# Queries and keys of batches 0 and 1 read in long runs, and the first layer's weights rebuilt two tiles at a time

## The chip, the cores and the metric

One core of one Trainium2 chip runs the whole kernel. The metric is the time of one execution on the device in microseconds. Before the change it was 829.93 us, the median of 3 runs (829.26 to 830.01). The profile comes from one further execution of the same program.

## The reference

Attention over 4 batches, 8 heads, 576 positions and 64 values per head feeds two layers of the same form. The attention adds a coarse part (queries, keys and values averaged by fours, a full softmax over 144 groups, repeated four times) and a local part (each position sees the three before and the three after it).

```python
q_d = q.reshape(B, H, Sd, factor, D).mean(axis=3)        # factor 4; k and v the same
out_up = np.repeat(sm_attn(q_d, k_d, v_d), factor, axis=2)
mask = np.abs(pos[:, None] - pos[None, :]) < factor
scores = np.where(mask, scale * q @ k.T, -1e9)
out = out_up + softmax(scores) @ v                       # float32
x = moe(out)      # h = x @ w_in;  max(0.01 h, h) @ w_out
x = moe2(x)       # h = x @ w_in;  a squared ramp of h;  @ w_out
```

There are 2304 rows; w_in is 512 by 2048 and w_out 2048 by 512, in both layers. q, k and v come as float32, the four weights as float64, of which the kernel reads the two 32-bit words.

## The kernel before

**The two layers.** The rows are cut into four blocks of 512 and one of 256. A weight is held as two float16 tiles (a high part and a remainder), and each product is three float16 products on PE. The first layer runs `g1` (L1939, x by w_in) and `g2` (L2203, by w_out) in steps of 12 products; one step of `g1` takes one of the 16 column tiles of w_in. The second layer (L1969, L2039, L2139) trades products for sums on DVE.

**A weight tile** is rebuilt in `weight` (L632): a DMA brings 64-bit words into a buffer (L667), DVE shifts and joins them in three instructions (L686, L692, L698) into a float32 tile of 512 elements, ACT rounds that to the high part (L723) and DVE takes the remainder (L756). There are 16 such tiles of w_in and 16 of w_out in the first layer. From the third tile of w_in on, one DMA already brings two tiles, but each is rebuilt by itself.

**The attention of batches 0 and 1** (of batch 1 the first 448 positions, for the local part) works on transposed queries and keys. `prep` (L1157) loads, for each batch and each of four pairs of heads, the queries and keys by blocks of 64 positions, with one DMA for each head (L1172): 64 partitions by 9 runs of 64 floats. `tr` (L1203) turns each block, both heads at once, by a transposing product with the identity: 64 partitions by 128 columns, nine of them, five into one bank of PSUM and four into another. `tr_c` (L1221, L1233) copies each bank to SBUF on ACT. The scores (L1512) and the products with the values (L1572) follow; the coarse part sums the transposed queries and keys by fours on DVE (L1310) and has its own scores (L1351), transposes (L1402) and products (L1420). The rest of the attention is done on DVE with rows on partitions (L1707 to L1816).

**The order** of all instructions is worked out while the program is built. Each piece of work is an entry with an engine, a duration, the buffers and banks that it needs and the entries that it waits for; a planner walks through time and gives each engine the ready entry of the lowest key. Engines issue strictly in that order. Where the plan finds nothing ready for PE up to 140 us of its own time, it writes a product of zeros into a spare bank (`fill`, L2548): 128 by 512, whose result is not used. There are 80 of these. The numbers of the plan that the change touches are the largest count of weight loads open at a time (AHEAD), the spacing of the attention's due times (HP_GAP), the priority of the local attention of later blocks (RUSH_P), and the assumed durations of the transposing products and of their copies.

The other way to load queries and keys stands in the program already, behind `b in RUNS`, with `RUNS = ()`, so that no batch uses it:

```python
if b in RUNS:
    nc.sync.dma_start(
        out=st[nm].ap[:QB].rearrange("p (h x) -> p h x", h=2),
        in_=src[b, 2 * hp:2 * hp + 2].rearrange("h (i n) d -> i h (n d)", n=QBB))
```

Of the kernel before, what the change touches and what calls it, by code (L numbers as in the profile page):

```python
# [59 lines left out]
RUSH_P = 8  # L60
# [16 lines left out]
RUNS = ()  # L77
# [23 lines left out]
HP_GAP = 0.8  # L101
# [3 lines left out]
TWO_FROM = {1: 2, 2: 99}  # L105
# [3 lines left out]
AHEAD = 4  # L109
# [300 lines left out]
def kernel(  # L410
# [138 lines left out]

    def per_step(blk):  # L550
        return BLK // tokens(blk)
# [69 lines left out]
    w_in[1] = [w1_rows[:, i].rearrange("p f (c n) -> p f c n", c=KDM) for i in range(2)]  # L621
# [10 lines left out]
    def weight(m, which, f, due):  # L632
        st = {}
        hi, lo = (e[:, f] for e in (w_in, w_out)[which][m])
        if which == 0:
            hi, lo = (e.rearrange("p c n -> p (c n)") for e in (hi, lo))
            src = w_src[m][0].rearrange("(c p) n -> p c n", p=P)[:, :, f * P:(f + 1) * P]
        else:
            src = w_src[m][1][f * P:(f + 1) * P, :]

        two = which == 0 and f >= TWO_FROM[m]
        second = two and (f - TWO_FROM[m]) % 2 == 1
        n_load = 2 if two else 1
        if second:
            st = w_two[m, f - 1]
        if which == 0:
            w_two[m, f] = st

        lead = LEAD_W if m == 2 else (LEAD_W1, LEAD_W1O)[which] + (W1_MORE if f >= W1_FROM else 0)
        ch = Chain(due, lead, 512 + (0 if second else 1024 * n_load), hold=RESERVE_W, early=m == 1)  # L650
        ch.window = WINDOW_W if m == 2 else WINDOW
        if m == 1 and f < W1_RUSH:
            ch.rush = RUSH

        def load():
            w_open[0] += n_load
            w_begun[m] += n_load
            st["s"] = buf(1024 * n_load, m == 1)
            st["users"] = n_load
            t = st["s"].ap.bitcast(I32)  # L660
            if which == 0:
                t = t.rearrange("p (c n) -> p c n", c=KDM)
                s = w_src[m][0].rearrange("(c p) n -> p c n", p=P)
                s = s[:, :, f * P:(f + n_load) * P].bitcast(I32)
            else:
                s = src.bitcast(I32)
            nc.sync.dma_start(out=t, in_=s)  # L667

        def words():
            a = st["s"].ap.bitcast(I32)  # L670
            if which == 0:
                a = a.rearrange("p (c n t) -> p c n t", c=KDM, t=2)
                a = a[:, :, P:] if second else a[:, :, 0:P]
                return a[:, :, :, 0], a[:, :, :, 1]
            a = a.rearrange("p (n t) -> p n t", t=2)
            return a[:, :, 0], a[:, :, 1]

        def f32(i32=False):
            a = st["f", f].ap
            a = a.bitcast(I32) if i32 else a  # L680
            return a.rearrange("p (c n) -> p c n", c=KDM) if i32 and which == 0 else a


        def c1():
            st["f", f] = buf(512, m == 1)
            nc.vector.tensor_scalar(  # L686
                out=f32(True), in0=words()[1], scalar1=3, scalar2=0x3FFFFFF8,
                op0=ALU.logical_shift_left, op1=ALU.bitwise_and,
            )

        def c2():
            nc.vector.scalar_tensor_tensor(  # L692
                out=f32(True), in0=words()[1], scalar=-0x40000000, in1=f32(True),
# [3 lines left out]
        def c3():  # L697
            nc.vector.scalar_tensor_tensor(  # L698
                out=f32(True), in0=words()[0], scalar=29, in1=f32(True),
# [3 lines left out]
        def loaded():  # L703
            st["users"] -= 1
            if not st["users"]:
                st["s"].free()
            w_open[0] -= 1

        late = (m, which) == (2, 1)
        if not second:  # L710
            o = ch.op("SP", DMA, load, [w_last[f - W_EARLY]] if late and f >= W_EARLY else [],
                      need=(1024 * n_load,),
                      lat=LAT_W[which] * n_load)
            o.gate = lambda: w_open[0] < AHEAD and (
                m == 1 or w_begun[1] == 2 * KFF and o.key <= sch.step + WINDOW_W
                and (which == 1 or arena.close_spare())
            )
            st["load"] = o
        old = [w_last[f]] if late else []
        ch.op("DVE", t_dve(512, True), c1, [st["load"]], need=(512,))  # L720
        ch.op("DVE", t_dve(512), c2)
        ch.op("DVE", t_dve(512), c3, after=(loaded,))
        ch.op("ACT", t_act(512), lambda: nc.scalar.activation(  # L723
            out=hi, in_=st["f", f].ap, func=AF.Copy, scale=SW), ch.ops[-1:] + old)
        free = (lambda: st["f", f].free(),)
        if m == 1 and f < LO_PE[which]:

            def low():
                ps = st["ps"] = banks.get()
                nc.tensor.matmul(ps, ident_w, st["f", f].ap, start=True, stop=False)  # L730
                nc.tensor.matmul(ps, ident_n, hi, start=False, stop=True)

            ch.op("PE", dict(dur=5 * t_mm(512), cols=5 * 512), low, banks=1, mlp=True,
                  after=free)
# [1849 lines left out]
```

## Time and profile before

| what | value |
|---|---|
| median of 3 runs | 829.93 us |
| profiled execution, its own time | 827.44 us |
| its span, first to last instruction | 825.7 us |
| PE busy | 815.7 us (99%) |
| DVE busy | 723.9 us (88%) |
| ACT busy | 488.5 us (59%) |
| DMA busy share, 0 to 40 us | 0.93 |
| packets under 512 bytes | 36062 of 74155 |

The busy time of PE counts every product, those of zeros too, and the ends of its products are modelled: a product of 512 columns is shown some 380 ns long, while in a row they start about 216 ns apart. So a share of 99% says that PE's stream has almost no holes, not that all of it is wanted work. What a group of products costs is read from where it starts to where the next group starts.

### The profile page before, as it was taken

What the parts mean: (1) busy time and instruction counts of PE and PEld (TensorE: products, weight loads), DVE (VectorE), ACT (ScalarE), POOL (GpSimd) and SP (SyncE); (2) the same over time, 40 slices, a digit from 0 to 9 for tenths busy, and PEclk for the clock granted to TensorE, in tenths of its full rate; (3) what the DMA queues carried; (4) which work ended last, traced back from release to release, by engine and by line L of the source; (5) the groups of instructions that cost most, each with busy time, mean ns of one, the idle gap of its engine ahead of it and who ended that gap; (6) DMA issues with size and microseconds to landing.
All of it is one profiled execution on the core that took longest, in us unless ns stands there. A gap on an engine that the chain in (4) does not pass through costs nothing. (4 is left out here: it accounts for less than half of the span.)

```text
span 825.7 us, 16297 instructions
## 1 busy us (share of the span) xinstructions
PE 815.7 (99%) x6244; PEld 542.8 (66%) x6244; DVE 723.9 (88%) x1347; ACT 488.5 (59%) x1258; POOL 38.9 (5%) x60
## 2 busy tenths in 40 slices
PE   8999999999999999999999999999999999999998
PEld 5765555444454445444447886766888888889997
DVE  5997999999999999999999999998598598858661
ACT  5977676473633564363545557776677576746640
POOL 2001000051002400000000000000000000000000
PEclk9999999999999999999999999999999999999999
DMA  9988746693226703401512333000100000000001
GB/s 153 181 196 189 221 148 208 169 171 60 58 68 160 118 1 92 126 1 51 154 52 102 103 109 108 40 1 1 52 1 15 23 18 2 14 27 14 2 21 58
DMA packets 74155, 67.88 MB, mean 82 GB/s; under 512 B 36062, under 2 KB 57950, under 8 KB 74078
## 3 DMA queue, kind: packets, MB, share of 16 engines
q1 hardware_dynamic: 62878, 62.69, 27.3%
q0 software_dynamic: 11200, 4.15, 4.4%
q8 instruction: 49, 0.80, 0.4%
q14 instruction: 28, 0.23, 0.1%
HBM read 62.08 MB, written 4.72 MB: 81 GB/s over the span
## 5 line engine op out<-in xcount | busy, mean ns | idle before, releaser
L1939 PE MATMUL bank<-arena,w 128*128 128x512 f16 (+1 forms) x960 | 197.3, 358 | 0.0
L2203 PE MATMUL bank<-arena,w 128*128 128x512 f16 (+1 forms) x912 | 193.1, 362 | 0.0
L1939 PEld LDWEIGHTS <-w 128*128 128x128 f16 x960 | 92.9, 98 | 88.5 <-issue 1.0
L2203 PEld LDWEIGHTS <-w 128*128 128x128 f16 x960 | 92.1, 98 | 87.2 <-issue 2.3
L2139 PEld LDWEIGHTS <-arena 128*128 128x128 f16 x930 | 90.7, 98 | 10.4
L1969 PEld LDWEIGHTS <-w 128*128 128x128 f16 x960 | 86.3, 98 | 14.0 <-issue 2.6
L1969 PE MATMUL bank<-arena,w 128*128 128x256 f16 (+1 forms) x768 | 93.2, 269 | 1.1 <-DVE bank L2019 0.6
L2139 PE MATMUL bank<-w,arena 128*128 128x256 f16 x600 | 75.3, 273 | 0.0
L2052 ACT ACTIVATE arena<-bank 128x512 f32<-128x512 f32 x67 | 39.7, 592 | 55.6 <-PE bank L1939 52.5
L1969 PEld LDWEIGHTS <-arena 128*128 128x128 f16 x720 | 64.8, 98 | 9.9 <-issue 0.4
L1969 PE MATMUL bank<-arena 128*128 128x256 f16 (+1 forms) x576 | 66.9, 264 | 0.2 <-DVE w L2064 0.2
L2182 DVE SCALAR_TENSOR_TENSOR arena<-arena 128x512 f16<-128x512 f32 x69 | 47.0, 684 | 2.6 <-ACT arena L2178 2.6
L2064 DVE SCALAR_TENSOR_TENSOR w<-w,bank 128x512 f32<-128x512 f32 x50 | 33.8, 681 | 17.6 <-ACT w L2060 17.2
L2056 ACT ACTIVATE w<-bank,half 128x512 f32<-128x512 f32 x50 | 34.2, 684 | 22.6 <-DVE bank L2019 19.3
L2178 ACT ACTIVATE arena<-arena 128x512 f16<-128x512 f32 x69 | 43.4, 629 | 1.2 <-DVE arena L1816 0.3
L2001 ACT COPY w<-bank 128x256 f32<-128x256 f32 x100 | 34.2, 366 | 15.5 <-PE bank L1969 14.7
L1782 DVE TENSOR_TENSOR arena<-arena 128x768 f32<-128x768 f32 (+2 forms) x60 | 41.1, 688 | 1.4
L2105 ACT ACTIVATE arena<-arena 128x256 f16<-128x256 f32 (+1 forms) x62 | 33.1, 556 | 13.2 <-DVE arena L2064 5.6
L1707 DVE TENSOR_TENSOR arena<-arena 128x1792 f32<-128x1792 f32 x20 | 40.2, 2016 | 0.6 <-issue 0.3
L2139 PE MATMUL bank<-arena 128*128 128x256 f16 x330 | 40.4, 273 | 0.0
L1715 DVE TENSOR_REDUCE arena<-arena 128x28 f32<-128x1792 f32 x20 | 40.1, 2009 | 0.0
L1763 ACT ACTIVATE arena<-arena 128x64 f32<-128x64 f32 x140 | 35.5, 338 | 7.6 <-DVE arena L1746 7.6
(251 smaller groups left out, 1335.3 us busy)
## 6 DMA issues: line engine op xcount, KB each, us to landing
arena<-in_moe_w_in_dram SPq DMA_DIRECT2D x15, 1024.0 KB
arena<-in_moe_w_out_dram SPq DMA_DIRECT2D x8, 1024.0 KB
arena<-in_moe_w_out_dram SPq DMA_DIRECT2D x10, 512.0 KB
w<-in_moe_w_out_dram SPq DMA_DIRECT2D x6, 512.0 KB
arena<-in_k_dram SPq DMA_DIRECT2D x23, 112.0 KB
arena<-in_v_dram SPq DMA_DIRECT2D x23, 112.0 KB
arena<-in_k_dram SPq DMA_DIRECT2D x16, 144.0 KB
out_dram<-w SPq DMA_DIRECT2D x9, 256.0 KB
```

The source lines that it names most:

```text
L1707: nc.vector.tensor_tensor(pv(par, j0), st["q", par].ap.rearrange("p (j d) -> p j d", d=D)[:, j0:j0 + JC, :] .unsqueeze(2).to_broadcast([P, ...
L1715: nc.vector.reduce_sum(sv(par)[:, j0:j0 + JC, :], pv(par, j0), axis=AX)
L1763: nc.scalar.activation(out=pr[:, j, w, :], in_=va[:, j0 + j + w, :], func=AF.Copy, scale=sv(par)[:, j0 + j, w:w + 1],)
L1782: nc.vector.tensor_tensor(out, x, y, op=ALU.add)
L1939: nc.tensor.matmul(h[:, e], a[:, f, c, :] if m == 1 else a[:, f // FP, c, f % FP], y[:, :, c, :], start=(n == 0), stop=(n == 3 * KDM - 1),)
L1969: nc.tensor.matmul(o[:, e], a[:, i, c], y[:, k, c, :], start=first and e == 0 and n == 0, stop=n == 5, skip_group_check=True,)
L2001: nc.scalar.copy(side(p, nm), part(p, t, j))
L2052: nc.scalar.activation(out=t, in_=st["h", p], func=AF.Prelu, scale=s_in * sg, alpha=0.01)
L2139: nc.tensor.matmul(o[:, k], a[:, i, at:at + P], y[:, j], start=opens and p == e == k == n == 0, stop=p == PH - 1 and e == E - 1 and n == 2 ...
L2178: nc.scalar.activation(out=gv(p)[0], in_=st["t", p].ap, func=AF.Copy, scale=so)
L2182: nc.vector.scalar_tensor_tensor(out=lo, in0=st["t", p].ap, scalar=so, in1=hi, op0=ALU.mult, op1=ALU.subtract)
L2203: nc.tensor.matmul(o, a, y[:, e, :], start=(first and n == 0 and c % E == 0), stop=(last and n == 2), skip_group_check=True,)
```

## The change

It does three things in the program, and gives the planner other numbers. First, `RUNS = (0, 1)`: for batches 0 and 1 partition i receives positions 9i to 9i+8 of both heads, in runs of 2304 bytes, by one DMA instead of two. The block that `tr` turns then holds every ninth position, and one head of it is turned by one ordinary product with the identity into its half of the bank's partitions, so that there are two products where one transposing product was. The copy on ACT writes the positions back in order (steps of nine). Second, tiles 2 to 15 of w_in of the first layer are rebuilt two at a time, by instructions of 1024 elements; w_in lies in another order in SBUF for that. Third, the lines that add 1e-9 and take the reciprocal become one helper, with the same instructions.

```diff
-RUSH_P = 8
+RUSH_P = 20
-RUNS = ()
+RUNS = (0,1)
+RUN_PE = 0.045
+RUN_ACT = 1.5
-HP_GAP = 0.8
+HP_GAP = 1.0
-TWO_FROM = {1: 2, 2: 99}
+TWO_FROM = (2, 98)
-AHEAD = 4
+AHEAD = 6
...
-    def weight(m, which, f, due):
+    def weight(which, f, n, due):
...
+        size = 512 * n
...
         def c1():
-            st["f", f] = buf(512, m == 1)
+            st["f"] = buf(size, True)
             nc.vector.tensor_scalar(
-                out=f32(True), in0=words()[1], scalar1=3, scalar2=0x3FFFFFF8,
+                out=f32(), in0=words()[1], scalar1=3, scalar2=0x3FFFFFF8,
...
-                        nc.tensor.transpose(
+                        nc.tensor.matmul(
                             ps[par * D:(par + 1) * D, (n - n0) * QB:(n - n0 + 1) * QB],
-                            a[:, par, n, :], ident[:QB, :QB]
+                            a[:, par, n, :], ident[:QB, :QB], start=True, stop=True,
                         )
...
-                t = ch.op("PE", pe_tr(QB, n * (2 if b in RUNS else 1), QB), ...
+                t = ch.op("PE", pe_mm(RUN_PE * 2 * n, QB, 2 * n, P) if b in RUNS else pe_tr(QB, n, QB), ...
-                c = ch.op("ACT", t_act(n * QB, True), ...
+                c = ch.op("ACT", t_act(n * QB, True) * (RUN_ACT if b in RUNS else 1), ...
...
+    for which, late in ((0, 0.0), (1, 1.5)):
+        f = 0
+        while f < KFF:
+            n = 2 if f >= TWO_FROM[which] else 1
+            weight(which, f, n, step_of[1, b0, f // per_step(b0)] + late)
+            f += n
```

PE's first rows after its opening products of zeros (nine before the change, seven after), first of the kernel before; L1216 is the transposing product, L2548 the zeros.

```order
L1216 MATMUL bank_64<-ident,w_61 128x64 x5
L2548 LDWEIGHTS zeros
L2548 MATMUL bank_63<-zeros 128x512
L2548 LDWEIGHTS zeros
L2548 MATMUL bank_63<-zeros 128x512
L2548 LDWEIGHTS zeros
L2548 MATMUL bank_63<-zeros 128x512
L1216 MATMUL bank_65<-ident,w_61 128x64 x4
L1216 MATMUL bank_66<-ident,w_61 128x64 x5
L1216 MATMUL bank_67<-ident,w_61 128x64 x4
```

The same place in the changed kernel; L1165 is the product with the identity, L2501 the zeros, L1451 and L1466 the local scores.

```order
L1165 MATMUL bank_64<-ident,w_61 64x64 x10
L1165 MATMUL bank_65<-ident,w_61 64x64 x8
L1165 MATMUL bank_66<-ident,w_61 64x64 x10
L1165 MATMUL bank_67<-ident,w_61 64x64 x8
L1165 MATMUL bank_68<-ident,w_61 64x64 x10
L1165 MATMUL bank_69<-ident,w_61 64x64 x8
L2501 LDWEIGHTS zeros
L2501 MATMUL bank_63<-zeros 128x512
L1451 LDWEIGHTS ident_72
L1451 MATMUL bank_70<-band,ident_72 128x280
```

Three loads are turned in one piece where before two were turned with zeros between. Over the whole program the transposing products (L1216) are 144 in 24 pieces before, the products with the identity (L1165) 288 in 21 pieces after, and the products of zeros 80 before and 46 after: of these 54 and 36 stand ahead of the first product of the first layer, 26 and 10 behind it.

On DVE, a stretch of the first layer's weights of the kernel before (L686, L692, L698 and L756 are the four instructions of a tile):

```order
L686 TENSOR_SCALAR w_61<-arena 128x512 x2
L1537 TENSOR_SCALAR w_61<-w_61 128x3
L1538 RECIPROCAL w_61<-w_61 128x3
L1602 SCALAR_TENSOR_TENSOR arena<-w_61,arena 128x192
L756 SCALAR_TENSOR_TENSOR w_81<-arena,w_81 128x512
L692 SCALAR_TENSOR_TENSOR w_61<-arena,w_61 128x512 x2
L1586 TENSOR_TENSOR w_61<-bank_63,arena 128x256
L698 SCALAR_TENSOR_TENSOR w_61<-arena,w_61 128x512 x2
```

And the first pair of w_in in the changed kernel (L682, L688, L694 and L710 are the same four):

```order
L682 TENSOR_SCALAR w_61<-arena 128x1024
L694 SCALAR_TENSOR_TENSOR w_61<-arena,w_61 128x512
L688 SCALAR_TENSOR_TENSOR w_61<-arena,w_61 128x1024
L553 TENSOR_SCALAR w_61<-w_61 128x4
L554 RECIPROCAL w_61<-w_61 128x4
L553 TENSOR_SCALAR w_61<-w_61 128x3
L554 RECIPROCAL w_61<-w_61 128x3
L1321 TENSOR_REDUCE w_61<-bank_64 72x2
```

One instruction of 1024 elements stands where two of 512 stood; the tiles of w_out keep their 512.

## Rows read from the trace of the kernel before

**Rows 1.** The page, part 1: busy time, share of the span, instructions.

```profile
PE 815.7 (99%) x6244; PEld 542.8 (66%) x6244; DVE 723.9 (88%) x1347; ACT 488.5 (59%) x1258; POOL 38.9 (5%) x60
```

**Rows 2.** Windows: length, busy us of PE, PEld, DVE, ACT, POOL, clock, DMA share, GB/s.

```profile
0.00:40.00 40.00, 37.81 (x438) 24.68 (x438) 29.68 (x102) 28.99 (x130) 4.16 (x22) 1.00 0.93 170
...
80.00:120.00 40.00, 40.00 (x314) 21.13 (x314) 38.23 (x89) 30.03 (x102) 1.56 (x3) 1.00 0.62 197
...
240.00:280.00 40.00, 40.00 (x202) 19.43 (x201) 39.29 (x59) 19.70 (x55) 11.04 (x10) 1.00 0.68 152
```

**Rows 3.** Waits of PE: for whom, us in total, times, longest.

```profile
PE bank L2039 <- DVE w L2182: 0.7, 1, 0.7
...
PE bank L1216 <- DMA w<-in_q_dram: 0.4, 1, 0.4
```

**Rows 4.** Timeline of the start: start, us, engine, line, operation.

```profile
0.75 1.41 SPq L1172 DMA_DIRECT2D w<-in_q_dram  x2
...
1.20 3.85 PE L2548 MATMUL bank<-zeros 128*128 128x512 bf16 x9 [1.20 <-DVE half L520]
...
5.07 0.49 PE L1216 MATMUL bank<-ident,w 64*128 64x64 f32 x5
```

**Rows 5.** Timeline of PE, 24 to 45 us.

```profile
24.93 0.77 PE L1216 MATMUL bank<-ident,w 64*128 64x64 f32 x9
25.64 0.69 PE L1572 MATMUL bank<-w 70*64 70x64 f32 x16
26.25 0.39 PE L2548 MATMUL bank<-zeros 128*128 128x512 bf16 x1
26.57 0.69 PE L1572 MATMUL bank<-w 70*64 70x64 f32 x16
27.19 0.39 PE L2548 MATMUL bank<-zeros 128*128 128x512 bf16 x1
27.42 0.60 PE L1555 MATMUL bank<-ident,w 128*70 128x128 f32 x4
...
28.07 0.71 PE L1512 MATMUL bank<-w 64*64 64x70 f32 x16
28.71 0.46 PE L1216 MATMUL bank<-ident,arena 64*128 64x64 f32 x4
...
42.60 1.15 PE L1572 MATMUL bank<-w,arena 70*64 70x64 f32 x32
43.68 0.39 PE L2548 MATMUL bank<-zeros 128*128 128x512 bf16 x1
43.91 0.41 PE L1402 MATMUL bank<-ident,w 72*72 72x72 f32 x4
44.26 0.52 PE L1216 MATMUL bank<-ident,arena 64*128 64x64 f32 x5
44.71 0.39 PE L2548 MATMUL bank<-zeros 128*128 128x512 bf16 x1
```

**Rows 6.** Weight loads of L1572: ns min/median/max, first and last start, forms.

```profile
L1572 PEld LDWEIGHTS bank<-w x92: 132/138/139, 25.6 to 148.8; 70*64 70x64 f32 x92
```

**Rows 7.** Timeline of DVE: two instructions of a tile in a row.

```profile
97.83 1.28 DVE L698 SCALAR_TENSOR_TENSOR w<-arena,w 128x512 int32<-128x512 int32 x2
```

**Rows 8.** DVE, line L954 of the second layer's weights: ns min/median/max.

```profile
L954 DVE SCALAR_TENSOR_TENSOR arena<-arena x11: 1210/1217/1227, 372.0 to 521.8; 128x1024 int32<-128x1024 int32 x11
```

**Rows 9.** ACT groups to 160 us: busy, mean ns, idle before.

```profile
L1233 ACT ACTIVATE w<-bank 128x320 f32<-128x320 f32 x13 | 5.7, 439 | 7.3 <-PE bank L1216 7.0
```

**Rows 10.** ACT with a stepped output (L1809) and without (L2178).

```profile
L1809 ACT ACTIVATE arena<-arena x10: 620/630/632, 245.9 to 393.5; 128x512 f16<-128x512 f32 x10
...
L2178 ACT ACTIVATE arena<-arena x69: 612/630/642, 57.7 to 537.4; 128x512 f16<-128x512 f32 x69
```

**Rows 11.** DMA, 0 to 20 us: packets and their sizes.

```profile
DMA packets 10449, 3.07 MB, mean 153 GB/s; under 512 B 9881, under 2 KB 10448, under 8 KB 10448
```

**Rows 12.** DMA, 72 to 76 us: packets and their sizes.

```profile
DMA packets 711, 1.39 MB, mean 347 GB/s; under 512 B 68, under 2 KB 141, under 8 KB 711
```

More of the change, by code (lines that the diff above doesn't have):

```diff
@@ L703, in loaded @@
         def loaded():
[L704 to L734, printed above, removed]
-            w_ready[m, which, f] = ch.op(
-                "ACT", t_act(512, True), lambda: nc.scalar.copy(lo, st["ps"]),
-                after=(lambda: banks.put(st["ps"]),))
-            ch.close()
-            return
@@ L740, in weight @@
-        if LO_DMA[m][0] <= f < LO_DMA[m][1]:
-            def neg():
-                st["n"] = buf(512, m == 1)
-                nc.scalar.activation(out=st["n"].ap, in_=hi, func=AF.Copy, scale=-1.0 / SW)
-            ch.op("ACT", t_act(512), neg, need=(512,))
-            ch.op("Pool", 1.05, lambda: nc.gpsimd.dma_start(
-                out=st["f", f].ap, in_=st["n"].ap, accum_op=ALU.add), lat=1.5,
-                after=(lambda: st["n"].free(),))
-            w_ready[m, which, f] = ch.op(
-                "ACT", t_act(512), lambda: nc.scalar.activation(
-                    out=lo, in_=st["f", f].ap, func=AF.Copy, scale=SW), after=free)
-            ch.close()
-            return
@@ L755, in weight @@
-        w_ready[m, which, f] = ch.op(
-            "DVE", t_dve(512), lambda: nc.vector.scalar_tensor_tensor(
-                out=lo, in0=st["f", f].ap, scalar=SW, in1=hi, op0=ALU.mult, op1=ALU.subtract),
-            after=free)
+            st["s"].free()
+            w_open[0] -= n
+        o = ch.op("SP", DMA, load, [], need=(1024 * n,), lat=LAT_W[which] * n)
+        o.gate = lambda: w_open[0] < AHEAD
+        ch.op("DVE", t_dve(size, True), c1, need=(size,))
+        ch.op("DVE", t_dve(size), c2)
@@ L759, in weight @@
+        ch.op("DVE", t_dve(size), c3, after=(loaded,))
+        ch.op("ACT", t_act(size), lambda: nc.scalar.activation(
+            out=hi, in_=tiles(), func=AF.Copy, scale=SW))
+        o = ch.op("DVE", t_dve(size), lambda: nc.vector.scalar_tensor_tensor(
+            out=lo, in0=tiles(), scalar=SW, in1=hi, op0=ALU.mult, op1=ALU.subtract),
+            after=(lambda: st["f"].free(),))
+        for e in fs:
+            w_ready[1, which, e] = o
         ch.close()
@@ L1378, in rec @@
         def rec():
[L1379 to L1381 removed]
+            inverse(st["ml"].ap[:GH, 4:8])
         def norm():
```

87 lines of the change are left out of this document (34 added, 53 removed).

## The prediction

> **What bounds the kernel now.** I read the page first: PE is busy 815.7 of 825.7 us [rows 1]. The windows then say whether that holds in every stage: in the first 40 us PE has holes of 2.2 us and the DMA engines are busy 0.93 of the time; from 80 us on PE has none, and DVE is nearly as full, 38.23 and 39.29 of 40 us [rows 2]. The waits of PE are short: once 0.4 us for queries at the start, and later 0.7 us at most, for DVE [rows 3]. So the end is set by PE's stream, by what stands in it and not by what it waits for, with DVE close behind from 80 us on. But 80 entries of that stream are products of zeros, put there because the plan had nothing else. The third view, PE's timeline, gives a price for each kind of entry: the distance from its start to the start of the next group, since the shown lengths overlap. So the time is forecast by changing the stream: what leaves it, what enters, and whether a wait opens where zeros stood.
>
> **Zeros that leave.** The order has 46 of them where 80 were, 7 instead of 9 in the opening. The nine of the opening start at 1.20 us and the first transpose at 5.07, which is 0.43 us each [rows 4]; two fewer give 0.9 us, if the first queries land by then. They should: before, two DMAs of 576 runs each are issued in 1.41 us [rows 4], and now one DMA of 128 runs does the same. The other 71 cost 0.23 us (27.19 to 27.42, 43.68 to 43.91) to 0.32 us (26.25 to 26.57) [rows 5]. I take 0.25, nearer to the low end, which is also what most of the 71 show; 32 fewer give 8.0 us. Together 8.9 us leave, with ends at 0.9 + 32 x 0.23 = 8.3 and 0.9 + 32 x 0.32 = 11.1.
>
> **Products that enter.** The transposes before: nine in one piece take 0.71 us (24.93 to 25.64), five 0.45 (44.26 to 44.71) [rows 5], so 0.065 each and 0.125 for a piece. 144 in 24 pieces cost 9.4 + 3.0 = 12.4 us. The 288 products with the identity are nowhere in this trace. The nearest row is the local product with the values, L1572: 64 columns, one head into each half of the output partitions, both heads read from the same input partitions, as in the new `tr`. 16 of its records take 0.61 us (25.64 to 26.25) and 32 take 1.08 (42.60 to 43.68) [rows 5], so 0.0294 a record and 0.14 for a piece. The order has 8 products where the trace has 16 records, so a product is two records, 0.0588 us. Then 288 in 21 pieces cost 16.9 + 2.9 = 19.8 us: 7.4 more than before. The bounds: if a product with the identity were one record, 8.5 + 2.9 = 11.4 us, 1.0 less than before; if the two heads did not overlap and each record took twice the time, 33.9 + 2.9 = 36.8 us, 24.4 more. I take 7.4, because L1572 has the same columns, type and pairing, and differs only in 70 input partitions against 64.
>
> A rule speaks against this price. The Trainium skill, "TensorE: Matmul & The Clock Gate", in "Part 3: Packing small matmuls — row/col tiling", says that a weight load overlaps running products only when its row group differs; here all 288 use the same rows. The same holds for L1572, whose loads last 138 ns [rows 6], and yet its records start 29 ns apart. L1512, whose heads do change the row group, is no faster: 16 records of 70 columns in 0.64 us (28.07 to 28.71) [rows 5]. So this trace does not show the rule at work; by the rule, 576 bare loads of 138 ns would add 79 us, 906.7 in all. I give that 0.01, as a part of rival 4.
>
> **Fewer breaks.** Up to the second layer PE's stream has 415 pieces before and 389 after. 17 of the 26 are zeros and 3 transposes, counted already. The other 6, at the 0.14 us of a piece, give 0.8 us.
>
> **The copies on ACT** read PSUM and write SBUF in steps. 32 of them, 0.439 us for 320 elements [rows 9]. A stepped output alone costs nothing: 630 ns with and without [rows 10]. A stepped read of PSUM is not in the trace; the same number of elements can hardly take less, and half as much again is the factor that the plan assumes, so the bounds are 0 and 0.22 us each, 7.0 in all. I take 0 on the path: ACT has 11 us free in the first 40 [rows 2], and the plan has already allowed for the longer copies. If that cover is missing, PE waits for them; that is in the third rival.
>
> **The DMAs.** Of the 74155 packets 18432 were 256-byte runs of these queries and keys (16 loads of 2 x 576), and they become 2048. In the first 20 us nearly all packets are under 512 bytes and 153 GB/s flow [rows 11]; where long runs dominate, 347 GB/s [rows 12]. That speeds up a resource that PE hardly waits for: PE's one wait on it was 0.4 us [rows 3]. It pays only through the zeros that the plan could drop, which are counted. SP issues 16 DMAs fewer in that queue. With up to six weight loads open instead of four, some of them stand earlier among the loads of the values; half a megabyte takes 1.5 us at 347 GB/s, and the short packets that are gone give back more than that.
>
> **The weights.** Seven pairs save four DVE instructions each. Two instructions of 512 take 1.28 us [rows 7], one of 1024 1.217 [rows 8], so 0.06 us each, 28 x 0.06 = 1.8 us of DVE, and 7 instructions of ACT. On PE's stream this is worth nothing by itself. It matters because DVE is as full as PE from 80 us on: PE's stream can only become shorter by 2 us if DVE's does not stay as long as it was. It gets 1.8 us shorter, and its chain starts 0.9 us earlier.
>
> **The sum.** 7.4 - 8.9 - 0.8 = -2.3 us; I leave out 0.1 for small new waits and take -2.2. Against the profiled execution (827.44 us) that is 825.2. The median of the runs lies 2.5 us above that execution, so the forecast in its terms is 829.9 - 2.2 = 827.7 us. With zeros at 0.23 to 0.32 and one break more or less, this case spans 825.5 to 829.5.
>
> **The rivals.**
> 1. *The new products cost less than L1572.* For it: identity and smaller tiles. Against it: L1512 has tiles of 64 by 64 too and is no quicker. One record each would give -1.0 - 8.9 - 0.8 = -10.7, 819.2 us; half way between, 823.5.
> 2. *The zeros go and waits come.* 26 zeros stood behind the first product of the first layer, where each step needs a tile that DVE has just rebuilt, and 10 stand there now. If DVE (38 of 40 us) or the copies on ACT deliver no sooner, PE waits for what it did not fill: 16 x 0.25 = 4.0 us come back as idle time, less the 1.8 us that DVE saves. Then -2.2 + 2.2 = 0: 829.9 us. For it: DVE's share. Against it: the new products keep PE some 7 us behind a plan that prices them at 0.045 us, so others are rather early.
> 3. *The opening runs at half pace for longer: slower.* The first nine products of zeros start 0.43 us apart, 512 columns at 1.2 GHz, although the clock column reads 1.00; later ones start 0.23 apart, 2.4 GHz. Now the opening is two shorter and 54 small products of 64 rows follow at once. If these leave PE at the lower pace until the first local scores, they cost 3.2 us more; with the copies on ACT at the upper bound for the first three loads, 6 x 0.22 = 1.3, PE's first part ends 4.5 us later: 832.2. It decides from 2.2 us on, some 37 products at half pace. Against it: before the change, transposes and zeros in turn kept the pace.
> 4. *The two heads do not overlap.* Price 24.4 instead of 7.4: +14.8, 844.7 us. For it stands a second rule of the Trainium skill, next paragraph; against it the rows of L1572.
>
> The Trainium skill, "FP8 and Floating Point Precision", "TensorE Precision Notes", says that a true float32 product takes four passes. Four passes of 64 columns at 2.4 GHz are 0.107 us (an estimate by that page), against the 0.0588 that L1572 shows, so the pairing of the halves seems to hide half of it there; 288 x 0.107 + 2.9 = 33.7 us would be 21 more than before.
>
> **Chances.** Forecast 0.41, rival 1 0.14, rival 2 0.25, rival 3 0.14, rival 4 0.06. A difference under 0.2%, 1.66 us, can't be told from none here. Faster by more: 0.8 of the forecast (0.33), all of rival 1 and 0.02 of rival 2, 0.49. Within: 0.08 and 0.18 of rival 2, 0.26. Slower: 0.05 of rival 2, and rivals 3 and 4, 0.25. The range of 8 in 10 reaches from 823, half way into rival 1, to 833, just above rival 3; rival 4 and the cheaper half of rival 1 are left out.
>
> **What would show it.** Products of zeros: 46, those behind the opening still 0.23 to 0.32 us. L1165: 18 products, 36 records, about 1.2 us from start to the next start; under 0.9 is rival 1, over 2 rival 4. The first of them at about 4.2 us; starts 0.06 us apart at 5 us are rival 3. L1189: 0.44 us for 320 elements, up to 0.66 if the stepped read costs. Idle time of PE from 50 to 160 us: under 1 us by the forecast, 2 or more by rival 2, with a wait for L710 or L1189. The forecast is wrong if PE's stream is shorter by over 4 us, or if the median comes above 829.5.

## The result and the profile after

The changed kernel takes 835.6 us (median of 11 runs, 829.91 to 841.6), the kernel before in the same session 829.93 (11 runs). The medians lie 5.7 us apart; the ratio, which is taken over all runs and not from the medians, is 1.0086, with a 95% interval from 1.0065 to 1.0106. So the kernel became slower, where 2.2 us of gain were forecast, and the time lies outside the stated range. The profiled execution of after took 835.60 us, its span is 833.8. Runs over 1.5% above the fastest of their kernel (one of e6, 857.25 us, and one of e16, 848.62, which is the profiled one) are left out of the medians below.

First the page and the windows of after, for [rows 1, 2] (columns as there):

```profile
PE 822.4 (99%) x6630; PEld 553.3 (66%) x6642; DVE 722.2 (87%) x1319; ACT 490.1 (59%) x1251; POOL 38.7 (5%) x60
...
PEclk6899999999999999999999999999999999999999
...
DMA packets 57519, 67.92 MB, mean 81 GB/s; under 512 B 17375, under 2 KB 39263, under 8 KB 57439
```

```profile
0.00:40.00 40.00, 36.91 (x494) 26.25 (x498) 21.50 (x70) 21.13 (x89) 4.16 (x22) 0.74 0.77 140
80.00:120.00 40.00, 40.00 (x331) 20.75 (x329) 38.65 (x77) 29.71 (x93) 1.45 (x5) 1.00 0.73 238
240.00:280.00 40.00, 39.88 (x194) 18.97 (x193) 39.55 (x51) 21.05 (x55) 8.31 (x7) 1.00 0.63 140
...
10.00:20.00 10.00, 9.52 (x106) 6.60 (x108) 5.80 (x17) 4.25 (x23) 0.26 (x4) 0.50 0.90 158
20.00:30.00 10.00, 9.94 (x103) 7.19 (x100) 3.63 (x12) 5.00 (x21) 0.00 (x0) 0.56 0.42 88
```

PE is as full as before, with 6.7 us more of busy time, and the two later windows look as before. What has changed is the clock of the first 40 us: 0.74 granted where 1.00 stood. In the second window of ten it is 0.50, 1.2 GHz, and a PE that counts as busy for 9.5 of 10 us does little more than half of what it does at 2.4. PE's timeline (start, length, line) shows it by the entries that [rows 4, 5] have:

```profile
1.20 3.17 PE L2501 MATMUL bank<-zeros 128*128 128x512 bf16 x7 [1.20 <-DVE half L522]
...
4.95 2.60 PE L1165 MATMUL bank<-ident,w 64*64 64x64 f32 x72 [0.57 <-DMA w<-in_q_dram]
7.90 1.91 PE L1165 MATMUL bank<-ident,w 64*64 64x64 f32 x36 [0.35 <-DMA w<-in_q_dram]
...
10.52 1.20 PE L1466 MATMUL bank<-w 64*64 64x70 f32 x16
...
15.86 2.19 PE L1165 MATMUL bank<-ident,w 64*64 64x64 f32 x36
...
30.04 1.26 PE L1165 MATMUL bank<-ident,w 64*64 64x64 f32 x36
31.24 0.82 PE L2501 MATMUL bank<-zeros 128*128 128x512 bf16 x3
...
63.24 0.94 PE L1307 MATMUL bank<-w 64*72 64x144 f32 x8 [0.32 <-DVE w L1266]
...
65.75 5.34 PE L1890 MATMUL bank<-arena,w 128*128 128x512 f16 x24 [0.38 <-ACT w L1484]
```

At 30.04 us 36 records of the new product take 1.20 us to the next start. At 15.86 the same 36 take 2.19. The local scores, 16 records, take 1.13 us from 10.52 to the next start, 0.64 before. The first product of the first layer starts at 65.75; before it was 54.24. From there to the end after takes 833.8 - 65.75 = 768.1 us and before 825.7 - 54.24 = 771.5. So the first layer starts 11.5 us later, and 3.4 of them come back behind it. Not all of the 11.5 is loss: with the change's planner numbers alone (e9 below) the first layer starts at 60.17, and that kernel ends sooner than before.

The chain of work that ended last (start, length, what) names something else beside the half pace:

```profile
53.36 8.02 DMA arena<-in_v_dram
...
61.75 0.68 DVE arena L694
62.43 0.66 DVE w L1266
...
65.75 5.34 PE bank L1890 x24
```

It is a load of values for the coarse part, issued by POOL at 53.36: of each four positions it adds the last two to the first two, which are in SBUF already (line 1248 here, L1292 before). It lands after 8.02 us, and the sums on DVE and the copies on ACT follow it. In this execution PE itself hardly stood still for it: on that chain it waits 0.32 us at 63.24 and 0.38 at 65.75 (the rows above), so here the late load cost 0.7 us at most. Before, the load at this place (line, form, duration of the issue on POOL, start; below it the time to landing) was issued at 49.6, landed after 4.6, and nobody waited for it:

```profile
L1292 POOL DMA_DIRECT2D w<-in_v_dram x1: 1315/1315/1315, 49.6 to 49.6; - x1
...
DMA to landing us min/median/max: 4.6/4.6/4.6
```

The copies on ACT (for [rows 9]), a step of the weights (for [rows 7, 8]) and the transfers of the first 20 us (for [rows 11]) in after; the first row gives busy us and mean ns, the second ns min/median/max, first and last start:

```profile
L1189 ACT ACTIVATE w<-bank 128x320 f32<-128x320 f32 x12 | 5.6, 470 | 5.3 <-PE bank L1165 5.2
```

```profile
L688 DVE SCALAR_TENSOR_TENSOR w<-arena,w x9: 657/686/1220, 51.1 to 150.7; 128x512 int32<-128x512 int32 x6, 128x1024 int32<-128x1024 int32 x3
```

```profile
DMA packets 4036, 3.08 MB, mean 154 GB/s; under 512 B 2667, under 2 KB 3243, under 8 KB 4035
```

A copy of 320 elements takes 470 ns on average against 439 before, and a pair takes 1.22 us where two singles took 1.28. The opening moves 3.08 MB in 4036 packets instead of 3.07 MB in 10449, at the same 154 GB/s: fewer packets did not bring more bytes.

### The profile page after: what moved, and what is told of

The parts are those of the page before. It is cut to its first block, busy times and chain, and to the rows that moved or that the text cites. A ratio compares the mean times of both kernels' runs of the same rounds, so it can differ in the third digit from the quotient of the medians.

```text
span 833.8 us, 16970 instructions
## 1 busy us (share of the span) xinstructions
PE 822.4 (99%) x6630; PEld 553.3 (66%) x6642; DVE 722.2 (87%) x1319; ACT 490.1 (59%) x1251; POOL 38.7 (5%) x60
## 4 chain that ended last, share of the span: by engine, by line
PE 71%; DVE 22%; issue 3%; DMA 2%; ACT 2%; SPq 0%; DVEq 0%; ACTq 0%; POOLq 0%
PE bank L1890 16%; PE bank L2090 15%; PE bank L2154 15%; PE bank L1920 15%; DVE arena L1733 2%; DVE arena L1667 2%; DVE arena L1659 2%; PE bank L1165 2%; DVE arena L2133 2%; DVE arena L1703 2%; PE bank L1990 2%; DMA arena<-in_v_dram 1%; PE bank L1466 1%; DVE w L929 1%; PE bank L1507 1%
## 5 line engine op out<-in xcount | busy, mean ns | idle before, releaser
L2090 PEld LDWEIGHTS <-arena 128*128 128x128 f16 x966 | 94.3, 98 | 10.8
L1920 PE MATMUL bank<-arena,w 128*128 128x256 f16 (+1 forms) x864 | 98.4, 264 | 1.1 <-DVE bank L1963 0.7
L2090 PE MATMUL bank<-w,arena 128*128 128x256 f16 x762 | 93.3, 273 | 0.0
L1920 PEld LDWEIGHTS <-arena 128*128 128x128 f16 x720 | 64.8, 98 | 10.5 <-issue 1.1
L1920 PE MATMUL bank<-arena 128*128 128x256 f16 (+1 forms) x528 | 64.4, 268 | 0.6 <-ACT w L1952 0.4
L2056 ACT ACTIVATE arena<-arena 128x256 f16<-128x256 f32 (+1 forms) x78 | 41.2, 554 | 18.8 <-DVE arena L2015 8.2
L2007 ACT ACTIVATE w<-bank,half 128x512 f32<-128x512 f32 x46 | 31.5, 685 | 31.5 <-DVE bank L1970 30.8
L2015 DVE SCALAR_TENSOR_TENSOR w<-w,bank 128x512 f32<-128x512 f32 x46 | 31.4, 685 | 18.8 <-ACT w L2011 18.4
L2060 DVE SCALAR_TENSOR_TENSOR arena<-arena 128x256 f16<-128x256 f32 (+1 forms) x78 | 44.3, 599 | 0.6 <-ACT arena L2056 0.5
```

The source lines that it names most:

```text
L1920: nc.tensor.matmul(o[:, e], a[:, i, c], y[:, k, c, :], start=first and e == 0 and n == 0, stop=n == 5, skip_group_check=True,)
L2056: nc.scalar.activation(out=left(p, part, q0, q1)[:, 0], in_=src(), func=AF.Copy, scale=so)
L2060: nc.vector.scalar_tensor_tensor(out=d[:, 1], in0=src(), scalar=so, in1=d[:, 0], op0=ALU.mult, op1=ALU.subtract)
L2090: nc.tensor.matmul(o[:, k], a[:, i, at:at + P], y[:, j], start=opens and p == e == k == n == 0, stop=p == PH - 1 and e == E - 1 and n == 2 ...
```

## The experiments

The theory at the start: the opening runs at half pace because products of zeros that held the clock are gone. Its rivals: zeros are mere filler, or the planner, by its new counts and numbers, came to a worse order. The kernel before ran again beside every experiment, with medians from 828.42 to 830.14 us. So a difference of medians between two experiments is open by some 1.5 us, and the distance of each from the kernel before of its own session is the safer number; the ratios are taken so.

**e1: zeros back.** After, with 18 products of zeros at the heads of its first pieces, order otherwise the same.

```diff
+def warm(ps, upto):
+    if warmed[0] < upto:
+        warmed[0] += 1
+        nc.tensor.matmul(ps, zeros[:, 0:P], zeros, start=True, stop=True)
...
             ps = st["ps", nm, i] = banks.get()
             if b in RUNS:
+                warm(ps, 12)
...
+            warm(ps, 18)
             s = ps[:, :cnt * KB]
```

> The changed kernel in the same order, with 18 products of zeros added at the head of its first 12 pieces of identity products and of its first local scores, in the bank that the piece then overwrites. Theory 1 (the clock: PE falls to 1.2 GHz at about 8 us because too little runs on it, and stays there for 20 us): the granted clock stays at 1.00 through the first 40 us, the first product of the first layer starts at about 60 us instead of 65.8 (9 to 10 us of half pace gone, 18 x 0.25 = 4.5 us of zeros added), and the time is 830 to 832 us. Theory 2 (the time went into PE's waits on loads, copies and DVE, the low clock is a side effect): the zeros only add, 838 to 840 us. Theory 3 (the identity products are dearer than priced): no change of the clock, 840 us.

Measured: median 835.25 of 7, 1.0067 [1.004, 1.0094], but in two groups: 830.38 and 830.96, the other five 834.86 to 836.02. The profiled run is 830.38; its clock is 1.00 where after has 0.50, and the first layer starts 4.8 us earlier than in after (a window and a row of the timeline of e1):

```profile
10.00:20.00 10.00, 9.06 (x149) 6.07 (x151) 5.83 (x18) 4.72 (x25) 0.26 (x4) 1.00 0.97 170
```

```profile
60.95 5.34 PE L1899 MATMUL bank<-arena,w 128*128 128x512 f16 x24
```

So zeros in the opening are not mere filler: with 18 more of them the clock stayed up and the first layer started earlier. But most executions gain nothing, at mean clocks of 0.994 to 1.000, so pace is not the only reason (and one run of after, 829.91, reaches the lower group without them). A second run of e1 (830.57, profiled) fell into the lower group again and tells nothing apart. What was expected of it:

> The same kernel as e1_zeros_back once more, for a second profile: most of its runs were 4.6 us slower than the profiled one, some of them with a mean granted clock of 1.00 in the record. Theory 1 (the clock): a slow run shows PE's small products at twice their spacing (16 records of local scores in 1.2 us instead of 0.64) in a part of the first 30 us, even where the record says 1.00, and its first product of the first layer starts at about 65 us instead of 60.9. Theory 2 (waits): the spacing is the fast one, and PE waits 4 to 5 us more, in one or two places. If the run is fast, nothing is told apart.

**e2: fewer zeros in the kernel before.** Nothing else changed.

```diff
         for ps in to:
-            nc.tensor.matmul(ps, zeros[:, 0:P], zeros, start=True, stop=True)
+            filled[0] += 1
+            if not 9 < filled[0] <= 33:
+                nc.tensor.matmul(ps, zeros[:, 0:P], zeros, start=True, stop=True)
```

> The kernel before in the same order, with 24 of its 80 products of zeros left out, the 10th to the 33rd, which run between about 5 and 24 us. Its loads and transposes are untouched. Theory 1 (the zeros hold the clock): the granted clock falls to 0.5 for part of the first 30 us, and the time rises by 3 to 9 us, to 833 to 839. Theory 2 (zeros are only filler): the clock stays at 1.00 and the time is 825 to 830 us.

Measured: 830.94 of 10, 1.004 [1.0015, 1.0066], in two groups: six at 829.78 to 830.98, four at 835.14 to 835.84. The mean clock is 0.98 to 0.99 in seven of the ten and 1.0 in three; the 16 runs of the kernel before beside them have 0.997 to 1.0. Windows of the profiled execution (830.89), then two of its waits of PE (us in total, times, longest):

```profile
10.00:20.00 10.00, 10.00 (x99) 7.77 (x98) 6.57 (x19) 6.06 (x31) 0.20 (x2) 0.50 0.81 123
20.00:30.00 10.00, 10.00 (x95) 7.98 (x95) 6.75 (x21) 6.86 (x34) 0.16 (x3) 0.59 0.68 139
```

```profile
PE bank L1216 <- DMA w<-in_q_dram: 1.5, 2, 0.8
...
PE bank L1216 <- DMA w<-in_k_dram: 1.1, 1, 1.1
```

24 zeros, about 6 us of the stream at 0.25, went, and the kernel became slower by 0.4%; the first layer starts at 58.02 instead of 54.24, and the granted clock fell to 0.50 where it was 1.00 [rows 2]. With nothing but zeros taken away, this shows that they held it, and more: PE now waits 2.6 us for queries and keys where it waited 0.4 [rows 3], so the zeros also kept it behind its loads. The median lies in neither range of the text: the clock fell as theory 1 says, but in six of the ten runs it cost little more than the missing zeros saved.

**e4: other counts for the planner.** The plan books a quarter of the activity for the new products, to make it write more zeros itself.

```diff
-                t = ch.op("PE", pe_mm(RUN_PE * 2 * n, QB, 2 * n, P) if b in RUNS ...
+                t = ch.op("PE", pe_mm(RUN_PE * 2 * n, QB, 2 * n, P // 4) if b in RUNS ...
```

> The changed kernel with one number of the plan changed: the activity that the plan books for the identity products, which decides where it puts zeros, is a quarter of what it was. The plan then has 57 products of zeros instead of 46. Theory 1 (the clock): granted clock 1.00 or nearly so in the first 40 us, and 827.7 + 11 x 0.25 = 830.5 us, 828 to 832. Theory 2 (waits) and theory 3 (dear products): 835 to 839 us, as the changed kernel or a little more.

Measured: 866.9, 1.0463. The plan came out different everywhere: PE is busy for 64.9 of the 80 us from 160 to 240. It isolates nothing, and shows that one changed count of the plan can cost 30 us through the order that it leads to.

**The parts alone: e5, e6, e8, e9, e16.** Each has some of the change's three parts (the planner's numbers, the pairs of weights, the long runs) and its own plan. Their edits in short:

```text
 e5: after           -RUNS = (0,1)   +RUNS = ()
 e8: as e5, and      -RUSH_P = 20 HP_GAP = 1.0 AHEAD = 6   +RUSH_P = 8 HP_GAP = 0.8 AHEAD = 4
 e6: before          -RUNS = ()      +RUNS = (0,1)   (and the products with the identity)
 e9: before          -RUSH_P = 8 HP_GAP = 0.8 AHEAD = 4    +RUSH_P = 20 HP_GAP = 1.0 AHEAD = 6
 e16: as e6, with the numbers of e9
```

> The changed kernel with the loads and transposes of before (two DMAs of 256-byte runs, one transposing product for both heads), so only the weights by twos and the plan's other numbers are left of the change; 82 products of zeros. Theory 1 (the clock, through the identity products without zeros): clock 1.00 throughout, and the time that of before less some of DVE's 1.8 us, 826 to 831. Theory 2 in the form that the plan's other numbers (six open loads, priorities, spacing) or the pairs open the waits: 833 us or more.

> The kernel before with the long runs and the identity products alone; weights and the plan's other numbers as before; 48 products of zeros. Theory 1 (the clock falls because identity products stand where zeros stood): clock below 1.00 in the first 30 us, 833 to 840 us. Theory 2 (the pairs or the plan's other numbers): 826 to 830 us.

> The weights of w_in by twos alone: the changed kernel with the loads and transposes and the plan's numbers of before. The plan has 104 products of zeros where the kernel before has 80. Theory 1, as a count of PE's stream: clock 1.00, 24 x 0.25 = 6 us more than before less what DVE saves, 833 to 836 us. If zeros fill only time in which PE would have waited, and DVE's 1.8 us are what counts: 826 to 829 us.

> The kernel before with the three planner numbers of the change alone (20, 1.0 and 6 for 8, 0.8 and 4); 74 products of zeros instead of 80, the short runs, the transposing products and the single tiles as before. If the numbers are harmless by themselves: 828 to 831 us, first layer at 53 to 55 us. If the numbers bring the first layer's start later by themselves (more local work ahead of it): first layer at 58 us or later and 833 us or more. The runs alone and the pairs alone came to 839.2 and 837.9, so no part alone is expected to give the 835.6 of the whole.

> The kernel before with the planner's numbers and the long runs of the change, without the pairs of weights; 47 products of zeros, the opening on PE word for word that of the changed kernel. If the pairs cost the time (numbers alone 827.0, numbers with pairs 834.9): 826 to 830 us. If the opening's pace does: 833 to 837 us, with a granted clock of 0.50 in the opening and the first layer at 64 us or later. If it is the long loads of the pairs that the values wait for, half pace in the opening and still 829 to 832.

| kernel | numbers | pairs | runs | zeros | us (median) | us above before, same session | ratio to before |
|---|---|---|---|---|---|---|---|
| before | | | | 80 | 829.93 of 11 | 0 | |
| e9 | x | | | 74 | 827.02 of 5 | -3.1 | 0.9956 [0.994, 0.9972] |
| e8 | | x | | 104 | 837.86 of 4 | 7.8 | 1.0107 [1.0086, 1.0127] |
| e6 | | | x | 48 | 839.16 of 3 | 9.1 | 1.011 [1.0094, 1.0127] |
| e5 | x | x | | 82 | 834.92 of 4 | 5.6 | 1.0078 [1.0053, 1.0103] |
| e16 | x | | x | 47 | 836.78 of 6 | 8.4 | 1.0108 [1.0071, 1.0145] |
| after | x | x | x | 46 | 835.6 of 11 | 5.7 | 1.0086 [1.0065, 1.0106] |

The parts do not add up: pairs cost 8 to 9 us beside the old numbers and beside the new ones (e8; e9 to e5), yet beside the runs they cost nothing (e16 to after). Each part makes another order, with other waits: PE waits for DVE four times in e8, 3.7 us in all, and four times in e6, 2.3 us in all. In e16, whose opening on PE is that of after, the executions at a mean clock of 1.0 take 833.75 to 834.12 and the others 839.44 to 843.72. So a lower clock goes with a longer time there too, but that the opening's pace is its reason is not shown; even those at 1.0 lie 5 us above the kernel before. That the pairs cost the time of the whole change is refuted, since without them it is no shorter. The numbers alone are the one version that beats both kernels. Its first layer starts at 60.17 us, 6 us later than before, and yet it ends sooner, so the start of the first layer may be compared only between kernels of the same order: from there to the end of the span it is 766.6 us in e9, 771.5 in before, 775.3 in e5 (start at 56.11), and 767.6 to 768.2 in e1, e10, e11 and after, which share one order. Pairs and runs together beside the old numbers were not tried.

**after, profiled a second time.**

> The changed kernel once more, for a second profile. Theory 1 (the clock): the time goes with the length of the stretch at 1.2 GHz; each 2 us at half pace cost 1 us of PE's stream, up to the 20 us of the first profile; a run near 830 us has no such stretch. Theory 2 (waits): the time goes with PE's idle time, at whatever clock.

One run, 836.31 us at a mean clock of 0.995, and another picture of the same kernel. Timeline of PE, then the windows:

```profile
4.88 6.02 PE L1165 MATMUL bank<-ident,w 64*64 64x64 f32 x108 [0.51 <-DMA w<-in_q_dram]
...
11.61 1.20 PE L1466 MATMUL bank<-w 64*64 64x70 f32 x16
...
14.04 0.71 PE L1307 MATMUL bank<-w 64*72 64x144 f32 x8
...
25.00 1.26 PE L1165 MATMUL bank<-ident,w 64*64 64x64 f32 x36
...
62.01 1.47 PE L1307 MATMUL bank<-w 64*72 64x144 f32 x8 [4.14 <-DVE w L1266]
...
65.53 6.76 PE L1890 MATMUL bank<-arena,w 128*128 128x512 f16 x24
```

```profile
10.00:12.00 2.00, 1.67 (x25) 1.24 (x24) 0.84 (x2) 0.89 (x2) 0.00 (x0) 1.00 1.04 122
...
48.00:52.00 4.00, 3.94 (x94) 3.35 (x93) 3.85 (x13) 3.97 (x15) 1.47 (x3) 1.00 1.07 217
...
58.00:60.00 2.00, 0.00 (x0) 0.00 (x0) 0.00 (x0) 0.00 (x0) 0.00 (x0) 1.00 1.06 223
60.00:62.00 2.00, 0.00 (x0) 0.02 (x1) 1.82 (x4) 0.63 (x1) 0.00 (x0) 0.90 1.03 198
62.00:64.00 2.00, 1.99 (x18) 1.63 (x20) 2.00 (x8) 1.77 (x9) 0.00 (x0) 0.50 0.19 46
...
66.00:68.00 2.00, 2.00 (x6) 0.70 (x5) 1.97 (x5) 1.85 (x8) 0.00 (x0) 0.50 0.43 98
```

Half pace ended here at 14 us instead of 29, and still the first layer starts at 65.53. PE waits 4.14 us ahead of 62.01. From 58 to 60 us no engine does anything, while the DMA engines are full; after that PE's clock is 0.50. The chain, and one wait of DVE (us in total, times, longest), name what all wait for:

```profile
39.18 10.00 DMA arena<-in_v_dram
...
49.91 10.25 DMA arena<-in_v_dram
...
62.01 1.47 PE bank L1307 x7
63.48 2.12 PE bank L1165 x36
65.60 6.69 PE bank L1890 x24
```

```profile
DVE w L1259 <- DMA arena<-in_v_dram: 6.7, 1, 6.7
```

The first half of the values takes 10.00 us to land and the load that adds the second half 10.25. DVE's sum of these values (L1259) waits for them, and behind it in DVE's order stands the sum (L1266) that PE's coarse scores need. Between them SP had issued two loads of w_out of 0.5 MB and one of w_in of 1 MB (from 41.87, 48.93 and 49.52). That these loads are what holds the values up is read from their place in the queue, and not shown by it. This gave the second theory, A: the opening ends at 65 us because sums of values land late behind other loads; half pace and late values are two reasons of which either alone is enough.

**e10 and e11: without the first two adding loads.** After and e1, each without them; the other queues are as there.

```diff
-                nc.gpsimd.dma_start(out=t, in_=view(src)(2 * D), accum_op=ALU.add)
+                added[0] += 1
+                if added[0] > 2:
+                    nc.gpsimd.dma_start(out=t, in_=view(src)(2 * D), accum_op=ALU.add)
```

> The changed kernel without the first two accumulating loads of values (their second halves are left out of the sums); same order on all other queues, no zeros put back, so that only the opening's pace is left of the two reasons. Theory A (either reason alone brings the first layer to 65 us): executions that fall to half pace for 20 us (mean clock near 0.988) stay at 834 to 836; those that keep the pace or lose it for 6 us come to 829 to 832, since nothing waits for the values; the profile shows which it was by the start of the first layer, 65 or 60 to 62 us. Rival (the pace costs nothing by itself, the values are the one cause): all executions at 829 to 831. Rival 2 (the values cost only where zeros were put back): median 835 to 836.

> The changed kernel with 18 products of zeros put back at the head of its first pieces (as in e1_zeros_back), and without the first two accumulating loads of values (their second halves are left out of the sums); order on all other queues as there. Theory A (where the clock holds, the stream comes to the second of these sums before its load has landed, and some executions wait there): the waiting executions go, all times within 2 us of the lowest, median 829 to 831, first product of the first layer at about 60 us. Rival (the executions of 835 us have another cause, the clock or the plan): median stays at 834 to 836, or two groups 4 to 5 us apart remain.

Measured for e10: 830.0 of 12, 1.0015 [0.9997, 1.0032]; eleven at 828.45 to 830.84 (mean clock 0.996 or 1.0) and one at 835.38, which alone has a mean clock of 0.988, that of after's first profile. For e11: 830.94 of 12, 1.0019 [1.0003, 1.0036]; ten at 830.44 to 831.37, two at 834.91 and 836.49. It lies 0.8 us above the kernel before of its session, where e1 lay 5.9 above. PE in e10:

```profile
4.99 6.03 PE L1167 MATMUL bank<-ident,w 64*64 64x64 f32 x108 [0.62 <-DMA w<-in_q_dram]
...
11.72 1.20 PE L1470 MATMUL bank<-w 64*64 64x70 f32 x16
...
60.41 5.35 PE L1894 MATMUL bank<-arena,w 128*128 128x512 f16 x24
```

Up to 14 us e10 is as slow as the second profile of after, and yet its first layer starts at 60.41 instead of 65.53. So the late values cost 5.1 us there. In the medians they cost 5.6 us (835.6 to 830.0), or 4.1 with each taken against the kernel before of its own session (5.7 and 1.6 above it). e10 takes away the wait for these loads and their traffic in one, and does not tell them apart.

The two profiles of after bear out that each reason alone is enough. The piece of 36 identity products that starts at 30.04 us in the first starts at 25.00 in the second, so the long half pace cost 5.0 us more than the short one. From that piece to the first layer it is 35.7 us in the first profile and 40.5 in the second, against 35.0 in e10 (from 25.39) and 35.6 in e1 (from 25.36). The first execution lost its time to the pace, the second to the values. Theory A holds, with a correction: the short form of half pace, up to 14 or 16 us, costs little, and only the long one, some 20 us, is enough by itself. By their mean clock two of the eleven runs of after (0.988 and 0.989) are of the first kind, and so is the one run of e10. That two runs of e11 stay high is not explained, and no high run of e1 and none of after from 837 us up was profiled.

**e13 and e14: the pair's load later.** After and e1, with the first 1 MB load of w_in behind the next loads of queries and keys.

```diff
-            nc.sync.dma_start(out=t, in_=a.bitcast(I32))
+            late = n == 2 and not which and not held[0]
+            held[0] += late
+            if late:
+                held.append(lambda: nc.sync.dma_start(out=t, in_=a.bitcast(I32)))
+            else:
+                nc.sync.dma_start(out=t, in_=a.bitcast(I32))
```

> The changed kernel with the 1 MB load of the first pair of w_in issued some 8 us later, no zeros put back. Theory A: two reasons bring the first layer to 65 us in turn, half pace in the opening or, where the pace holds, the late values; only the second goes, so that the executions at half pace keep 834 to 836 and the others come to 830 to 832. Rival (the load of the pair is the one cause): median 830 to 831, in all executions. Rival 2 (the clock is the one cause): median 835 to 836 unchanged.

> As e1_zeros_back, but the 1 MB load of the first pair of w_in is issued behind the next loads of queries and keys, some 8 us later; nothing is left out. Theory A: the second accumulating load of values lands in 6 us or less instead of up to 10, DVE's wait in front of its sum falls from 1.7 to 6.7 us to under 1.5, and the median is 829 to 831; the weights are wanted at 62 us at the earliest and cost under 1 us. Rival 1 (the load of the pair isn't what the values wait for): median 834 to 836 as before. Rival 2 (the pair is late and DVE waits for it): PE or DVE wait for L717's weights 2 us or more, 832 to 837.

Measured: e13 837.13 of 4, 1.0076 [1.0054, 1.0099]; e14 838.58 of 6, 1.0105 [1.0085, 1.0126]. In e13 the first layer starts earliest of all versions of after's order: with the megabyte away, the values are in time, with half pace up to some 15 us and no zeros put back. But the pair is then late itself (a row of the timeline of PE in e13, and one of the waits of DVE: us in total, times, longest):

```profile
59.72 5.35 PE L1901 MATMUL bank<-arena,w 128*128 128x512 f16 x24
```

```profile
DVE w L689 <- DMA arena<-in_moe_w_in_dram: 7.8, 1, 7.8
```

The wait moves from the values to the weights, and PE stands still for 6.0 us behind the first 24 products of the first layer. That is rival 2 of e14's text; e13's text had no such rival, and its time lies in none of the ranges there. In the profile of e14 the values were late even so (one wait of DVE for them, 3.3 us, first layer at 62.33), so the megabyte is not the only load that holds them up. Neither place for it is free.

**e19: e16 with the 18 zeros of e1.**

> As e16_no_pairs, in the same order, with 18 products of zeros put back at the heads of the first pieces. If the opening's pace costs e16_no_pairs its time: 3 to 6 us less than that, 829 to 832, and the first layer at 59 to 61 us. If zeros are only filler: 18 x 0.25 = 4.5 us more than that. By the stream, from the numbers alone (827.0): products +7.4, 9 zeros fewer -2.3, so 832 us.

Measured: 837.72 of 4, 1.0106 [1.0075, 1.0137]: neither the gain nor the cost that was expected can be told from e16 (1.0108). The start of the first layer came to 61.22 us, just above the 59 to 61 expected; from there to the end it is 833.9 - 61.22 = 772.7 us, 6 more than in e9. So the greater part of what this order costs lies behind the opening.

## Why the prediction was wrong

- **The DMAs** are the step that failed. I put them at nothing on two grounds: PE hardly waits for a transfer, and half a megabyte of weights ahead of the values takes 1.5 us at 347 GB/s, less than the short packets give back. The first is a reading of before, where zeros kept PE behind the loads: without 24 of them its wait for queries and keys went from 0.4 to 2.6 us (e2). The second takes its rate from a stretch of long runs [rows 12]; around the values' loads the DMA engines are busy 1.0 of the time at some 200 GB/s. At that rate the 2 MB of weights issued from 41.9 to 50.8 us are 10 us, an estimate that equals what either load of the values took. Measured price of the late values: 4 to 6 us (after against e10). That the weights ahead of them make them late is shown in part only: moving one of them put the values in time in e13 and not in e14. The larger count of open loads does not do it by itself: e9 has it, its adding load lands in 5.8 us, and it is faster than before.
- **Zeros that leave**: not even the whole length of 8.9 us left the stream. The 0.9 of the opening shrank to 0.1, since PE then waited 0.57 us for the first queries (first product at 4.95, where 5.07 stood and 4.2 was forecast). And length was the wrong measure: the zeros held the clock and kept PE behind the transfers (e2). I named waits that take their place as rival 2, but looked for them at L710 and L1189 and priced 2.2 us. The wait that came, 4.14 us in the second profile, was for another instruction of DVE (L1266), which stood behind the sum of the late values.
- **Rival 3**, the opening at half pace, was the right mechanism at a chance of 0.14, and its evidence against (transposes and zeros kept the pace) was the reason for it: what kept the pace was to be removed. That its price of 4.5 us is near the 5.0 us that the long half pace cost beyond the short one is luck: I priced 54 products and slower copies, and in after everything from 8 to 29 us ran at 1.2 GHz.
- **Products that enter**: right. 36 records take 1.20 us at 2.4 GHz, against 1.2 forecast. The Trainium skill, "TensorE: Matmul & The Clock Gate", "Part 3: Packing small matmuls — row/col tiling", says that a weight load overlaps running products only when its row group differs; this does not show here either: all 36 use the same rows and start 33 ns apart, while one of their loads lasts 135 ns.
- **The copies on ACT**: 470 ns on average, +7%, and no wait of PE for them; right. **The weights** on DVE: 1.22 for 1.28 us, right as a duration; what the pairs do to the order was not foreseen (e8, 7.8 us above before).
- **The sum**: with the late values taken away the kernel takes 830.0, 1.6 us more than the kernel before of that session, where 2.2 less were forecast. So some 3.8 us of the forecast are missing there as well. Half pace up to 16 us lies in them; no run separates the rest. Behind the start of the first layer the span is 3.4 us shorter than before, but this does not bear out the count of zeros, products and breaks: with the planner numbers alone it is 4.9 us shorter (e9). What those numbers do by themselves, a gain of 3.1 us, was in no term of the sum. Also, its own terms span 825.3 to 828.4 us, and not 825.5 to 829.5.
- **What to look for**: PE's idle time from 50 to 160 us was 1.4 us in the first profile, between the signs of the forecast and of rival 2, and over 4 in the second, with L1266 on DVE at the end of the wait and not L710 or L1189.

## What to carry to other kernels

An instruction without use may still do two things, as e2 shows: hold the clock, and hold its engine behind its transfers; before its time is counted as gain, ask what the next instruction will find when it comes earlier. A resource that nobody waits for is not a free one: with its share near 1 an earlier consumer can meet it at once, and a load put in front is better priced at the rate of that stretch. Two profiles of one kernel can have two causes: compare the distance from one piece of work to the next, as from the 36 products to the first layer here, before one is named. Where a planner writes the order, test its new numbers alone: here they were worth 3.1 us, and all that was put on them cost more.

## What was not expected of the hardware

- The clock's column reads 1.00 in the first 15 us of after's second profile, while 108 records take 6.02 us (3.6 at 2.4 GHz) and 16 records 1.13 to the next start instead of 0.64. In the opening the pace is read from the distance of starts, not from that column.
- The same instruction order came to two states of the opening: pace kept until 8 us and then lost to 29; never reached until 14. One run of 11 has a mean clock of 1.0 and took 829.91, but e10's profile has 1.0 too and half pace until 16, so its opening is not known.
- The kernel before varies with its clock as well: beside e10 its eight runs at a mean of 0.996 to 0.998 take 829.70 to 831.88 us and the twelve at 0.999 or 1.0 take 826.61 to 828.91.
- After 4.1 us in which PE waited, the granted clock is 0.50 from 62 to 68 us, so a wait is paid a second time: the first 24 products of the first layer take 6.76 us instead of 5.34.
- An adding load of 144 KB took 4.6 us to land in before, 6.6 in e1, 8.02 and 10.25 in after: the same instruction, with other work and other transfers under way.
